# Reading the attention output projection's matrix four rows at a time, with each row still written to its own partition

## The chip, the core and the metric

The kernel runs on one core of one Trainium2 chip. The metric is the device time of one execution in microseconds (us), as a median over several executions.

Two short names help below. A *read* is what a DMA engine fetches from DRAM as one piece, and a *write* is what it puts into on-chip memory (SBUF) as one piece; *descriptor* is the author's word for the entry that describes such a piece; the traces show none. Of the engines, PE multiplies matrices, DVE works on vectors, and SP issues the copies. The trace records DMA *packets*.

## The reference, cut to what matters

```python
def _A_ref(x, k_cache, v_cache, wq, wo):          # decode attention, one query per batch
    ...                                           # window W = 2048 of 8192 positions, 16 KV heads, 32 query heads
    return o.transpose(...).reshape(B, Sq, Hq * Dh) @ wo      # wo: [4096, 576] bf16, 4.7 MB
# b = an MLP of 576 -> 4608 -> 576 with weights w1 and w2;  result = g * a + (1 - g) * b
```

K and V of the window are 134 MB of the 154.3 MB that are read. The output projection `wo` is 4.7 MB, or 3.1%.

## The kernel before

Everything big is loaded by SP's DMA queue, in one stream, into a ring of nine slots of 16 KB per partition. A K or V copy is 2 MB in 128 pieces of 16384 B. After every eighth V copy comes a chunk of `wo`: 1024 rows of 1152 B. Row `128 t + p` goes to partition `p`, block `t`, because that is the layout that the kernel's matmul takes.

```python
WOP, WO_CH, NSLOT = 768, 8, 9     # a block of 576 columns stands every 768 elements; 8 blocks in a chunk
def wo_chunk(i):
    s = take_slot()
    h0 = WO_CH * i
    dst = slot(s)[:, 0:WO_CH * WOP].rearrange("p (t c) -> p t c", t=WO_CH)
    d = dma("sp", lambda e: e.dma_start(dst[:, :, 0:D], A_wo[128 * h0:128 * (h0 + WO_CH), :].rearrange("(t p) c -> p t c", p=128)),
            "s%d" % s, WO_CH * 128 * D * 2, deps=slot_free[s], name="d_wo%d" % i, after=last_dma[-1:])
    last_dma.append(d)
    ...                           # matmuls of the chunk; the slot is free when they are done

def src_of(cache, g, q):          # K and V: 16 KB from each of 32 x 4 places
    hkv, b0 = 2 * g + q // 2, 4 * (q % 2)
    return cache[b0:b0 + 4, hkv, S0:Sk, :].rearrange("a (x r) d -> x a (r d)", x=32)
```

## Time and profile before

| | before |
|---|---|
| time, median | 369.5 us |
| span of the profiled run | 367.9 us |
| DMA queue of SP, packet time as a share of 16 engines' span | 98.9% |
| PE, DVE busy | 72%, 57% |

These are lines of the page of the kernel before. The first two rows have a value for each of 40 equal slices of the span: the busy share of the 16 DMA engines in tenths, and what they moved. Below them are the packets and SP's queue (packets, MB, share).

```profile
DMA  8999999999999999999999999999999999999994
GB/s 345 428 412 424 435 430 433 428 428 428 433 429 431 422 433 426 428 435 427 433 431 433 408 434 432 429 426 433 433 436 428 414 434 424 431 433 440 402 429 193
DMA packets 14923, 154.59 MB, mean 420 GB/s; under 512 B 1292, under 2 KB 5428, under 8 KB 6072
q1 hardware_dynamic: 14848, 154.29, 98.9%
```

The row DMA is full from end to end, so the DMA engines bound this kernel. The table of waits (us in total, times, longest) confirms it from the other side: DVE waits for K.

```profile
DVE arena L642 <- DMA arena<-in_A_k_cache_dram: 60.1, 15, 10.5
```

The timeline of SP around the first `wo` copy (start, duration, instruction): the K copy issued after it holds SP for 18.53 us.

```profile
95.16 0.54 SPq L675 DMA_DIRECT2D arena<-in_A_v_cache_dram  x1
95.74 0.59 SPq L723 DMA_DIRECT2D arena<-in_A_wo_dram  x1
107.98 18.53 SPq L627 DMA_DIRECT2D arena<-in_A_k_cache_dram  x1
126.56 0.82 SPq L675 DMA_DIRECT2D arena<-in_A_v_cache_dram  x1
```

All issues of the `wo` copy together (duration in ns: least, median, most):

```profile
L723 SPq DMA_DIRECT2D arena<-in_A_wo_dram x4: 373/378/586, 95.7 to 314.8; - x4
```

The trace also holds every DMA packet with start, duration and size. Grouped by size, the kernel before has:

```
size      packets   median ns   what
 1152 B     4104         51     rows of wo (4096 of them)
 4608 B      256        178     rest of w1, a part of w2
10368 B      384        389     w2
16384 B     8192        611     K and V
```

### The profile page before, as it was taken

What the parts mean: (1) busy time and instruction counts of PE and PEld (TensorE: products, weight loads), DVE (VectorE), ACT (ScalarE), POOL (GpSimd) and SP (SyncE); (2) the same over time, 40 slices, a digit from 0 to 9 for tenths busy, and PEclk for the clock granted to TensorE, in tenths of its full rate; (3) what the DMA queues carried; (4) which work ended last, traced back from release to release, by engine and by line L of the source; (5) the groups of instructions that cost most, each with busy time, mean ns of one, the idle gap of its engine ahead of it and who ended that gap; (6) DMA issues with size and microseconds to landing.
All of it is one profiled execution on the core that took longest, in us unless ns stands there. A gap on an engine that the chain in (4) does not pass through costs nothing.

```text
span 367.9 us, 4129 instructions
## 1 busy us (share of the span) xinstructions
PE 263.5 (72%) x1837; PEld 87.0 (24%) x1429; DVE 210.4 (57%) x253; ACT 47.8 (13%) x117; POOL 37.5 (10%) x163
## 2 busy tenths in 40 slices
PE   0349984797698589773986399774976398773984
PEld 0339200122132022110321032110321032113542
DVE  0704599699686665459654674469544775364000
ACT  1010000210300220003000310003100300003200
POOL 7020011012011002000101002010110000000000
PEclk9999999699599869887897869886996879886659
DMA  8999999999999999999999999999999999999994
GB/s 345 428 412 424 435 430 433 428 428 428 433 429 431 422 433 426 428 435 427 433 431 433 408 434 432 429 426 433 433 436 428 414 434 424 431 433 440 402 429 193
DMA packets 14923, 154.59 MB, mean 420 GB/s; under 512 B 1292, under 2 KB 5428, under 8 KB 6072
## 3 DMA queue, kind: packets, MB, share of 16 engines
q1 hardware_dynamic: 14848, 154.29, 98.9%
q8 instruction: 13, 0.21, 0.2%
q10 hardware_dynamic: 56, 0.03, 0.0%
q14 instruction: 6, 0.05, 0.0%
HBM read 154.31 MB, written 0.01 MB: 419 GB/s over the span
## 4 chain that ended last, share of the span: by engine, by line
DMA 61%; PE 20%; DVE 16%; SPq 1%; issue 1%; ACT 0%; DVEq 0%; ACTq 0%
DMA arena<-in_A_k_cache_dram 50%; DMA arena<-in_B_w_dram 11%; DVE arena L642 10%; PE ps L173 9%; PE ps L659 3%; DVE arena L587 3%; PE ps L498 2%; PE ps L682 2%; PE ps L697 2%; DVE arena L606 1%; DVE arena L590 1%; PE ps L500 1%; SPq L675 1%; DVE arena L596 0%; SPq L746 0%
## 5 line engine op out<-in xcount | busy, mean ns | idle before, releaser
L642 DVE STREAM_TRANSPOSE arena<-arena 128x2048 f32<-128x2048 f32 x64 | 145.5, 2299 | 71.1 <-DMA arena<-in_A_k_cache_dram 60.1
L173 PE MATMUL ps<-arena 128*128 128x512 bf16 x408 | 141.3, 462 | 0.0
L659 PE MATMUL ps<-arena 128*128 128x512 bf16 x128 | 58.8, 459 | 21.4 <-DVE arena L642 21.3
L691 ACT ACTIVATE arena<-ps 128x512 f32<-128x512 f32 x32 | 19.1, 598 | 196.8 <-PE ps L682 196.8
L659 PEld LDWEIGHTS ps<-arena 128*128 128x128 bf16 x128 | 15.0, 117 | 124.6 <-issue 71.3
L635 POOL COPY arena<-arena 32x32 bf16<-32x32 bf16 x128 | 26.0, 203 | 159.8 <-PE ps L173 145.2
L697 PE MATMUL ps<-arena 128*128 128x8 f32 x256 | 35.3, 269 | 8.7 <-ACT arena L691 7.7
L697 PEld LDWEIGHTS ps<-arena 128*128 128x128 f32 x256 | 34.0, 208 | 21.8 <-ACT arena L691 15.2
L682 PE MATMUL ps<-arena 128*32 128x512 bf16 x512 | 36.4, 410 | 2.9 <-DMA arena<-in_A_v_cache_dram 2.9
L651 PE MATMUL ps<-arena 128*128 128x512 bf16 x8 | 4.7, 585 | 40.8 <-DVE arena L606 40.8
L587 DVE TENSOR_REDUCE arena<-ps 128x1 f32<-128x2048 f32 x8 | 18.3, 2282 | 21.6 <-PE ps L173 21.6
L601 ACT ACTIVATE arena<-ps,arena 128x512 bf16<-128x512 f32 x32 | 21.6, 686 | 40.9 <-DVE arena L596 40.9
L606 DVE STREAM_TRANSPOSE arena<-arena 128x512 bf16<-128x512 bf16 x32 | 19.9, 674 | 0.9 <-ACT arena L601 0.9
L682 PEld LDWEIGHTS ps<-arena 128*32 128x32 bf16 x512 | 11.3, 100 | 37.4 <-issue 27.1
L715 POOL TENSOR_TENSOR arena<-arena 128x16 bf16<-128x16 f32 x15 | 4.0, 266 | 141.7 <-ACT arena L707 141.7
L498 PE MATMUL ps<-arena 128*128 128x8 bf16 x144 | 10.9, 201 | 4.7 <-DMA arena<-in_B_w_dram 4.7
L541 PE MATMUL ps<-arena 128*8 128x288 bf16 (+1 forms) x140 | 11.9, 316 | 2.9 <-DMA arena<-in_B_w_dram 2.8
L498 PEld LDWEIGHTS ps<-arena 128*128 128x128 bf16 x144 | 10.8, 157 | 5.2 <-DMA arena<-in_B_w_dram 5.2
L651 PEld LDWEIGHTS ps<-arena 128*128 128x128 bf16 x8 | 0.9, 107 | 45.1 <-DVE arena L606 45.1
L613 DVE RECIPROCAL arena<-ps 128x32 f32<-128x32 f32 x8 | 2.9, 358 | 13.9 <-PE ps L611 13.9
L420 PE MATMUL ps<-arena 8*128 8x8 bf16 x8 | 0.5, 167 | 13.4 <-DVE arena L393 9.7
L715 DVE TENSOR_TENSOR arena<-ps,arena 128x16 bf16<-128x16 f32 x1 | 0.2, 229 | 16.7 <-PE ps L697 16.7
(83 smaller groups left out, 97.1 us busy)
## 6 DMA issues: line engine op xcount, KB each, us to landing
arena<-in_A_k_cache_dram SPq DMA_DIRECT2D x32, 2048.0 KB, 33.3
arena<-in_A_v_cache_dram SPq DMA_DIRECT2D x32, 2048.0 KB, 34.1
arena<-in_B_w_dram SPq DMA_DIRECT2D x1, 4608.0 KB, 24.3
arena<-in_A_wo_dram SPq DMA_DIRECT2D x4, 1152.0 KB, 36.6
arena<-in_A_wq_dram SPq DMA_DIRECT2D x1, 4096.0 KB, 13.0
arena<-in_B_w_dram SPq DMA_DIRECT2D x3, 1296.0 KB, 14.8
arena<-in_B_w_dram SPq DMA_DIRECT2D x2, 576.0 KB, 20.6
arena<-in_A_wq_dram SPq DMA_DIRECT2D x1, 512.0 KB, 3.6
```

The costliest lines, as they stand in the source:

```text
L173: return e.add_instruction(mybir.InstMatmult(name=nc.get_next_instruction_name(), engine=mybir.EngineType.PE, ins=[e.lower_ap(rhs), e.lowe ...
L498: ins = e.matmul(out_, lhsT, yT[:, kt, :], start=(kt == 0), stop=False)
L541: ins = e.matmul(ps[32 * j:32 * j + 8, BK_ACC, 0:JN], lhsT, rhs[:, JN * j:JN * j + JN], start=False, stop=True, skip_group_check=True, til ...
L587: mx = add("dve", lambda e: e.tensor_reduce(out=k(MX), in_=ps[:, 0:4, :].rearrange("p a n -> p (a n)"), axis=AXL.X, op=ALU.max), deps=[qk_ ...
L601: return e.activation(out=Pm[:, 512 * c:512 * c + 512], in_=ps[:, c, :], func=ACTF.Exp, bias=k(NB), scale=SCALE, accum_out=k(SUM + c))
L606: pts.append(add("dve", (lambda c=c: lambda e: e.transpose(bass.AP(arena, offset=aoffs("PT") + 2048 * (g % 2) + 128 * c, ap=[[AST, 128], [ ...
L635: return e.tensor_copy(dst, src)
L642: tr = add("dve", (lambda h=h, kb=kb: lambda e: e.transpose(bass.AP(arena_f, offset=foffs("KT") + kb * 2048, ap=[[AST // 2, 128], [1, 2048]]),
L659: mm = e.matmul(*args, start=False, stop=last) if rc == 0 else held_matmul(nc, e, *args, stop=last)
L682: mm = e.matmul(ps[c:c + 32, BK_OS[i % 2], :], PT[:, g % 2, 512 * q + 32 * t:512 * q + 32 * t + 32], slot(s)[:, 512 * t:512 * t + 512], st ...
L691: u_ev[i] = add("act", lambda e: e.activation(out=EV[:, i % 2, :], in_=ps[:, BK_OS[i % 2], :], func=ACTF.Copy), deps=[prev] + ([u_sum[i - ...
L697: mm = e.matmul(ps[:, BK_S, OC + 16 * (item % 2) + 8 * (q % 2):OC + 16 * (item % 2) + 8 * (q % 2) + 8], EV[:, i % 2, 128 * r:128 * r + 128 ...
```

## The change

Four consecutive rows of `wo` are contiguous in DRAM. The change reads them as one piece of 4608 B. The four writes of 1152 B that follow must go to four partitions. The change gives the walk of the destination through a shape register, with `run_dma`; in the trace of the changed kernel this is one MOVE_SHAPE more for each copy (24 ns; 375 ns once). The intent is fewer and larger descriptors for the same layout on chip.

```diff
+def run_dma(nc, e, out, in_, shape=None):
+    ...  # turns the walk into numbers
+        kw = dict(dst_dge_shape=enc, bass_dst_dge_shape=tuple(walk))
+    return e.add_instruction(mybir.InstDMACopy(..., ins=e.lower_ap_dma(in_), outs=e.lower_ap_dma(out), **kw))
...
-            d = dma("sp", lambda e: e.dma_start(dst[:, :, 0:D], A_wo[128 * h0:128 * (h0 + WO_CH), :].rearrange("(t p) c -> p t c", p=128)),
+            src = bass.AP(A_wo.tensor, offset=128 * h0 * D, ap=[[4 * D, 32], [128 * D, WO_CH], [1, 4 * D]])
+            d = dma("sp", lambda e: run_dma(nc, e, dst[:, :, 0:D], src, (AST, ((4 * AST, 32), (WOP, WO_CH), (AST, 4), (1, D)))),
```

More of the change, by code (lines that the diff above doesn't have):

```diff
@@ L177, in held_matmul @@
         tile_size=tile_size, tile_position=tile_position, ldweights=False))
+def run_dma(nc, e, out, in_, shape=None):
+    item = 2
+    kw = {}
+    if shape is not None:
+        pst = shape[0]
+        walk = shape[1]
+        enc = []
+        for step, num in reversed(walk[:-1]):
+            parts, rest = divmod(step, pst)
+            assert parts == 0 or rest == 0
+            enc += [parts * 262144 + rest * item, num]
+        enc += [0, 1] * (4 - len(enc) // 2)
+        kw = dict(dst_dge_shape=enc, bass_dst_dge_shape=tuple(walk))
+    return e.add_instruction(mybir.InstDMACopy(
+        name=nc.get_next_instruction_name(), engine=e.engine, queue="qSPDynamicHW", mode="Copy",
+        ins=e.lower_ap_dma(in_), outs=e.lower_ap_dma(out), **kw))
 def build_kernel(nc, A_x, A_k_cache, A_v_cache, A_wq, A_wo, B_x, B_w1, B_b1, B_w2, B_b2, gate_w, out):
```

## The prediction

The sum came to 369.5 - 1.2 = 368.3 us, and the 1.2 us are the choice between 1.7 us, 0.8 us and nothing. The upper end of the range, 370.0 us, allows for causes of a slower time.

> **What bounds the kernel.** The 16 DMA engines. On the page, the row DMA shows nine tenths or more in every slice but the first and last, at 402 to 440 GB/s, and the SP queue's packets take 98.9% of the engines' span of 367.9 us; adding the packets' times up in 2 us steps of the trace, the engines are 99.7% busy from 2 us to 362 us. PE (72%) and DVE (57%) wait for data: in the table of waits DVE waits 60.1 us for K. So packet time saved is span saved.
>
> **What a row costs now.** The trace's DMA packets, grouped by size: 4104 of 1152 B take 51.1 ns each, 4096 of them the projection's rows: 4096 x 51.1 / 16 = 13.1 us of the 16 engines, 3.6% of the span for 3.1% of the bytes. Packets of 4608 B take a median of 178 ns, of 10368 B 389, of 16384 B 611. All fit a rate of 27.2 B/ns plus about 8.6 ns a packet. [...]
>
> **What the change does.** 4096 reads of 1152 B become 1024 of 4608 B; the 4096 writes of 1152 B stay; bytes, layout and order too. If the cost goes with the read, a quad falls from 4 x 51.1 = 204 ns to 178: 1024 x 26.4 / 16 = 1.7 us less. If it goes with the write, nothing. If both carry some, about 0.8 us. I lean to the read, and expect about 1.2 us.
>
> **What it adds.** Four times a shape register is loaded on SP, whose issues of these copies take 0.38 us (median) with slack around them; none of it should reach the critical path. [...]
>
> **The stall on SP.** Each time, the K copy after a projection copy holds SP for 18.5 to 22.3 us (timeline), and the first w2 copy 27 us, until just before the projection packets start (127.8 us for the first). It looks as if its 64 writes per engine fill the queue; K and V have 8. If writes count, the stall stays; I expect this (60%). If it shrinks, issue is earlier, but the engines are already 99.7% busy, so it buys next to nothing.
>
> **Time.** 369.5 - 1.2 = 368.3 us, range 367.3 to 370.0. Faster by over 2%: 0.01; within 2%: 0.97; slower by over 2%: 0.02.
>
> **What would show each step right or wrong.** Right: about 3,000 fewer packets on the page (14923 to about 11850), "under 2 KB" falling from 5428 to about 1350, new 4608 B packets near 178 ns; K, V and w2 packets unchanged at 611 and 389 ns; the row DMA still full. Wrong: 4608 B packets of about 204 ns (the writes carry the cost), or packets still counted as 1152 B at 51 ns.
>
> **What would make the prediction wrong.** [...]the engines run dry around the four projection copies (a dip in the row DMA at 128, 209, 289 and 346 us); fewer than 16 engines used; [...]packets over 204 ns or slower K packets beside them. These make it slower.

## The result

The changed kernel takes 369.19 us (369.02 to 369.38, 5 runs) against 369.51 us (369.37 to 369.71, 5 runs). The ratio is 0.9992, with a 95% interval of 0.998 to 1.0004. A ratio is the mean time of one kernel's fast runs over that of the other's of the same rounds, so it is not quite the ratio of the medians quoted. The gain is about 0.3 us, and its interval includes zero. A change this small has to be judged from packets, which repeat better than the time does: summed up as under x_r1w1 below, the packets of two kernels that move the same pieces in another order agree within 0.02 us (before and e4_split, x_r1w1 and bb_r1w1), while the runs of one kernel spread over some 0.35 us.

These are the same lines of the page after:

```profile
DMA  8999999999999999999999999999999999999994
GB/s 345 428 408 428 428 427 433 432 426 432 435 430 432 422 427 430 432 439 431 426 430 428 422 438 427 430 426 428 433 430 430 428 431 426 433 428 432 418 424 191
DMA packets 11851, 154.59 MB, mean 421 GB/s; under 512 B 1292, under 2 KB 1332, under 8 KB 3000
q1 hardware_dynamic: 11776, 154.29, 98.6%
```

There are 3072 packets fewer, as four reads became one. The bytes are the same, and the engines are still busy throughout. SP's timeline after, in the same stretch:

```profile
94.86 0.53 SPq L693 DMA_DIRECT2D arena<-in_A_v_cache_dram  x1
95.85 0.73 SPq L193 DMA_DIRECT2D arena<-in_A_wo_dram  x1
108.40 0.56 SPq L645 DMA_DIRECT2D arena<-in_A_k_cache_dram  x1
109.01 0.60 SPq L693 DMA_DIRECT2D arena<-in_A_v_cache_dram  x1
```

The long stalls are gone. The K copies after the first three `wo` copies held SP for 18.53, 22.29 and 21.89 us before, and 0.56, 0.54 and 0.53 us after. The issue of the `wo` copies (duration in ns: least, median, most) became dearer, which costs nothing here:

```profile
L193 SPq MOVE_SHAPE arena<-in_A_wo_dram x4: 24/24/375, 95.4 to 314.8; - x4
L193 SPq DMA_DIRECT2D arena<-in_A_wo_dram x4: 707/707/732, 95.8 to 314.9; - x4
```

So stalls of some 60 us in all went away, 3072 packets went away, and the time moved by 0.3 us. Two things in the packet records explain the size. The records do not name the engine, so I joined packets into the succession of one engine by their times; where two engines run in step, the joining can mix them.

**First, packets overlap.** An engine starts the next packet 4 ns before the record of the last one ends. A 51 ns packet starts every 47 ns, a 178 ns packet every 174, and a 611 ns packet every 607. What a packet costs the engine is the distance of starts, not its recorded duration.

**Second, some of the new packets are slow, always in the same places.** These are typical successions of one engine, size:duration in ns, with "x" for repeats; the first is of the kernel before, cut to one engine's 64 rows:

```
before: 16384:611 ... 1152:51 x64                                          16384:611 16384:611 ...
after:  16384:611 ... 4608:178 x11 4608:179 4608:193 4608:194 x3           16384:636 16384:611 ...
```

About the first eleven packets of a copy take 178 ns, the last four about 194, and then the first K packet takes 633 to 641 instead of 611 (some have 616 after it). Over all engines about 30% of the new packets take 184 ns or more, and there are 48 K packets of 630 to 645 ns, 16 for each of the first three copies, where the kernel before has none. 194 ns is a start every 190 ns, or 47.5 ns for each of the four writes. That is what a row cost before.

**Theory A.** A write of 1152 B costs about 47.5 ns, however wide the read was. A wide read can run ahead of its writes, but only until the room between is full. From the after trace this lead is some 11.5 x (190 - 174) = 184 ns, an estimate. Then reads go at the pace of the writes. What this room is, bytes or pieces or time, the trace does not say. When the copy ends, the next K packet waits, and part of the lead is given back.

**Rivals.** D: only the number of reads counts, at 8.6 ns each, as predicted, and something else ate the gain. B: the shape register, or the engines and partitions that it pairs, makes the slow packets (F is its form for the partition steps). C: a fixed number of write descriptors, 48 (the writes of the first twelve packets of the succession above, 12 x 4), is ready beforehand, and the rest comes at 47.5 ns each. E: the gain is the vanished stall.

### The profile page after: what moved, and what is told of

The parts are those of the page before. It is cut to its first block, busy times and chain, and to the rows that moved or that the text cites. A ratio compares the mean times of both kernels' runs of the same rounds, so it can differ in the third digit from the quotient of the medians.

```text
span 367.5 us, 4111 instructions
## 1 busy us (share of the span) xinstructions
PE 254.8 (69%) x1815; PEld 87.3 (24%) x1429; DVE 210.1 (57%) x253; ACT 47.8 (13%) x117; POOL 37.6 (10%) x163
## 4 chain that ended last, share of the span: by engine, by line
DMA 74%; DVE 12%; PE 11%; SPq 1%; ACT 1%; issue 1%; DVEq 0%; ACTq 0%
DMA arena<-in_A_k_cache_dram 50%; DMA arena<-in_B_w_dram 15%; DMA arena<-in_A_v_cache_dram 9%; DVE arena L660 9%; PE ps L173 5%; PE ps L516 2%; PE ps L677 1%; DVE arena L605 1%; PE ps L700 1%; SPq L765 1%; ACT arena L619 1%; DVE arena L624 1%; PE ps L518 1%; PE ps L715 1%; DVE arena L614 0%
## 5 line engine op out<-in xcount | busy, mean ns | idle before, releaser
L173 PE MATMUL ps<-arena 128*128 128x512 bf16 x401 | 134.4, 445 | 15.3 <-DVE arena L660 9.8
L677 PE MATMUL ps<-arena 128*128 128x512 bf16 x115 | 51.8, 450 | 16.7 <-DVE arena L660 16.6
L715 PE MATMUL ps<-arena 128*128 128x8 f32 x256 | 36.9, 275 | 8.7 <-ACT arena L709 7.7
L715 PEld LDWEIGHTS ps<-arena 128*128 128x128 f32 x256 | 35.6, 217 | 22.4 <-ACT arena L709 16.4
L669 PE MATMUL ps<-arena 128*128 128x512 bf16 x6 | 3.5, 585 | 37.8 <-DVE arena L624 37.8
L700 PEld LDWEIGHTS ps<-arena 128*32 128x32 bf16 x512 | 11.3, 100 | 39.8 <-issue 24.1
```

The source lines that it names most:

```text
L173: return e.add_instruction(mybir.InstMatmult(name=nc.get_next_instruction_name(), engine=mybir.EngineType.PE, ins=[e.lower_ap(rhs), e.lowe ...
L677: mm = e.matmul(*args, start=False, stop=last) if rc == 0 else held_matmul(nc, e, *args, stop=last)
L700: mm = e.matmul(ps[c:c + 32, BK_OS[i % 2], :], PT[:, g % 2, 512 * q + 32 * t:512 * q + 32 * t + 32], slot(s)[:, 512 * t:512 * t + 512], st ...
L715: mm = e.matmul(ps[:, BK_S, OC + 16 * (item % 2) + 8 * (q % 2):OC + 16 * (item % 2) + 8 * (q % 2) + 8], EV[:, i % 2, 128 * r:128 * r + 128 ...
```

## The experiments

### Shape registers in new kernels: three that were not run

Three variants of the changed kernel (a shape register with reads of one row, and reads of two and of eight rows) were refused before they reached the chip: new kernels may not set shape registers by hand. They gave no result. What they were to tell is on record, and later runs ask the same questions without the register:

> Shape register kept, but reads go back to one row of 1152 B. Theory A (read overhead is saved, writes stay at about 47 ns each, so reads can only run ahead of writes by some 190 ns per engine and copy): packets back at 1152 B and 51 ns, starting every 47 ns, time as before, 369.5 us within 0.2. If the number of reads fills the queue, the K copy after each projection copy holds SP for 18 to 22 us again; if it was the shape register that removed the stall, it does not. Rival B (the shape register or its engine assignment is what moved the time): time stays at 369.2 us or moves otherwise, or packets differ from 51 ns.

> Two rows per read (2304 B, 2048 packets). Theory A: a read could start every 89 ns, its two writes need about 95, so the lead grows by 6 ns a packet and reaches 190 ns only at the end of the 32 packets of an engine: nearly all packets take 93 ns, no slow ones at the end of a copy; gain much as with four rows, 369.2 us within 0.2. Rival C (the first 48 write descriptors of an engine are ready beforehand, and the rest come at 47.5 ns each): packets slow down to about 99 ns after the 24th of an engine. Rival D (only the number of reads counts, overhead 8.6 ns each): 1.1 us less than before, 368.4 us. Stall on SP: 32 reads per engine, expected short or gone.

> Eight rows per read (9216 B, 512 packets). Theory A: a read could start every 343 ns, its eight writes need about 380; lead of 190 ns is used up after about 5 packets, so packets 6 to 8 of an engine take about 384 ns instead of 347; gain per copy and engine at most 190 ns, as with four rows, 369.2 us within 0.2. Rival D (only the number of reads counts, 8.6 ns each): all packets at 347 ns, 2 us less than before, 367.5 us. Rival C: slow after the 6th packet, so not told apart from A here.

### The old copy in four parts (e4_split)

```diff
-            d = dma("sp", lambda e: e.dma_start(dst[:, :, 0:D], A_wo[... 1024 rows ...]...), ...)
+            for t in range(0, WO_CH, 2):
+                d = dma("sp", ... dst[:, t:t + 2, 0:D], A_wo[... 256 rows ...] ...)
```

> The old copy, in four copies of two heads each, 16 reads and writes per engine in each. Theory A: the 18 to 22 us stalls of SP are gone or short, packets stay at 51 ns, and the time stays at 369.5 us within 0.2, because the engines were busy through the stall anyway. Rival E (the gain of the change came from the stall that vanished): 369.2 us or less.

Measured: 369.66 us (5 runs), ratio 1.0005 (0.9992 to 1.0019). The expectation on the stall was wrong: it only moved, as SP's timeline of this kernel shows.

```profile
95.61 21.65 SPq L724 DMA_DIRECT2D arena<-in_A_wo_dram  x4
117.35 9.02 SPq L627 DMA_DIRECT2D arena<-in_A_k_cache_dram  x1
126.42 0.82 SPq L675 DMA_DIRECT2D arena<-in_A_v_cache_dram  x1
```

The four parts are stuck one behind the other, until the packets of `wo` start at 127.6 us. So the size of one copy is not what holds SP. In all, as many pieces wait as before; reads and writes are equally many here, so this run does not tell which of them count, if it is their number. Of rival E this run says nothing, as the stall is still there.

### Twelve more copies, in three forms (x_r1w1, x_r4w1, x_r4w4)

One copy's gain is below what a time can show, so these kernels add twelve copies of a chunk, spread over the stream, into slots that nobody reads. Results stay correct. The forms differ in the pieces read and written. None uses a shape register; the writes of a read go to one partition, and a copy with differing pieces is made as the instruction, with the two patterns given separately.

```diff
+def copy_as_given(nc, e, out, in_):
+    return e.add_instruction(mybir.InstDMACopy(..., ins=e.lower_ap_dma(in_), outs=e.lower_ap_dma(out)))
+        def wo_again(form):
+            s = take_slot()
+            rows_out = ...  # 128 partitions x 8 blocks of 1152 B, 1536 B apart
+            wide_out = ...  # 128 partitions x 2 blocks of 4608 B, 6144 B apart
+            rows_in = bass.AP(o, offset=0, ap=[[D, 128], [128 * D, 8], [1, D]])
+            four_in = bass.AP(o, offset=0, ap=[[4 * D, 32], [128 * D, 8], [1, 4 * D]])
+            # r1w1: rows_in -> rows_out   r4w1: four_in -> rows_out   r4w4: four_in -> wide_out
+            d = dma("sp", lambda e: copy_as_given(nc, e, dst, src), ..., deps=slot_free[s], ...)
+            slot_free[s] = [d]
```

> The kernel before with 12 more copies of a projection chunk, spread over the stream, into slots that nobody reads (results stay right); each in the old form, 64 reads and 64 writes of 1152 B per engine. This is the yardstick of the next two. All theories: packets of 51 ns every 47 ns, about 3.0 us a copy, so about 369.5 + 12 x 3.1 = 407 us. If the stalls of SP, now 16 instead of 4, run the queue dry, the DMA row dips and it is longer.

> As x_r1w1, but the 12 extra copies read 4608 B and write 1152 B, without a shape register: the four writes go to one partition, 1536 B apart. Theory A (each write of 1152 B takes about 47 ns, so reads only run ahead by some 190 ns per engine and copy, of which the next K packet gives back 25): first 11 packets of an engine 178 ns, the last 194, next K packet about 636; 12 x (0.16 - 0.025) = 1.6 us less than x_r1w1. Rival D (only the number of reads counts, 8.6 ns each, as predicted): 12 x 0.42 = 5 us less. Rival F (the slow packets come from stepping partitions in the shape register walk): no slow packets here, all 178 ns, 12 x 0.22 = 2.7 us less.

> As x_r1w1, but the 12 extra copies read 4608 B and write 4608 B into one partition. Theory A: no write is short, so all packets 178 ns, one every 174 ns, none slow, next K packet 611; 64 x 47 - 16 x 174 = 224 ns less per engine and copy, 12 x 0.224 = 2.7 us less than x_r1w1, a good us less than x_r4w1. Rival D: 5 us less than x_r1w1 and the same as x_r4w1.

All three ran on the same chip in the same rounds:

| | median us (runs) | less than x_r1w1 | sum of packet starts' distances / 16 | less |
|---|---|---|---|---|
| x_r1w1 | 405.77 (4) | | 371.87 us | |
| x_r4w1 | 404.80 (4) | 0.97 us | 370.96 us | 0.91 us |
| x_r4w4 | 403.08 (5) | 2.69 us | 369.16 us | 2.71 us |

The fourth column adds (duration - 4 ns) over all packets of SP's queue of at least 512 B that start after 25 us, and divides by 16 engines. The 128 packets of w1 that end before 28 us are left out, as the limit of 25 us cuts them differently in each trace. For the two kernels of the study the same sum is 335.79 us before and 335.35 after, 0.45 us less, beside a measured 0.3.

When reads and writes are both wide, the gain is 2.69 us, which is what the distance of starts gives: 12 x (64 x 47 - 16 x 174) ns = 2.69 us. (That it fits to the hundredth is luck: the runs of one of these kernels spread over 0.2 to 0.4 us.) All packets of its extra copies take 178 ns. When only the reads are wide, about a third of that is left, and the slow packets are back without a shape register and without stepping partitions: 178 x11, then 184 to 198, then a K packet of 636 ns. That refutes D, which wanted 5 us in both, and it clears the shape register (B, F): slow packets come without it. The gain in time of x_r4w1 was smaller than the 1.6 us expected: in this form many engines turn slow sooner (29 to 75% of a copy's packets take 184 ns or more, against 28 to 35% in the changed kernel); why is open.

The yardstick also bears on the stall. These lines are of the page of x_r1w1 (the row DMA in 40 slices, and the packets), then of its SP timeline:

```profile
DMA  8999999999999999999999999999999999999995
DMA packets 27403, 168.74 MB, mean 418 GB/s; under 512 B 1484, under 2 KB 17908, under 8 KB 18552
```

```profile
48.34 17.10 SPq L635 DMA_DIRECT2D arena<-in_A_k_cache_dram  x1
65.53 3.04 SPq L683 DMA_DIRECT2D arena<-in_A_v_cache_dram  x1
```

The same stretch of x_r4w1, with 16 reads per engine in the copy instead of 64, and the same 64 writes:

```profile
48.37 0.55 SPq L635 DMA_DIRECT2D arena<-in_A_k_cache_dram  x1
52.83 0.53 SPq L683 DMA_DIRECT2D arena<-in_A_v_cache_dram  x1
```

So fewer reads make the stall go away, with a shape register or without. But reads are not all that counts. After the other extra copies of x_r4w1 the next issue was held for up to 7.8 us, and after the last two for 11.3 and 14.2 us; in x_r4w4, with as many reads and only 16 writes, for at most 4.1 us. (Stalls of 17 to 26 us in both follow the four old copies.) In the bursts of bb_r4w1 below, the third copy of each burst was held for 14.0, 26.7, 26.9 and 23.1 us. Counting from the order of issues and the packets' ends, some 76 reads per engine waited when the K copy of the kernel before was let go, but only about 40 when the third copy of a burst was (estimates). So reads alone do not set the limit, and writes alone do not either: in the changed kernel up to 121 writes per engine waited without a stall of over 5 us, and in the kernel before 76 were enough for 18 (the same way of counting). What the limit is stays open. This is the third copy of the second burst in SP's timeline of bb_r4w1:

```profile
154.10 26.69 SPq L181 DMA_DIRECT2D arena<-in_A_wo_dram  x1
```

The stall costs nothing here: in x_r1w1 SP is stuck for most of the span, the row DMA stays full, and twelve copies cost 405.77 - 369.59 = 36.2 us, which is 12 x 64 x 47 ns = 36.1 us of packets and nothing more. E falls.

### A look at other forms (m1_mix)

```diff
-    twelve copies of one form                                        # in words
+    r4w1, r4w2, r4w4, r2w1, r8w1, two r4w1 back to back, r4w2, r4w4, r2w1, r8w1, r4w1, r8w4   # rows per read, rows per write
```

> One look at packets. The kernel before with extra copies of a projection chunk of several forms, into slots nobody reads: read 4608 and write 1152 (once two of these back to back), read 4608 and write 2304, read 4608 and write 4608, read 2304 and write 1152, read 9216 and write 1152, read 9216 and write 4608. Theory A (the lead of reads over writes is limited to about 190 ns, by the amount of data between): read 2304 write 1152 stays at 93 ns to the 32nd packet or nearly; read 9216 write 1152 slows from 347 to about 384 ns after about 5 of 8; read 4608 write 2304 gains lead at some 6 ns a packet and hardly slows; the second of the two copies back to back is slow (194 ns) from its first packet. Rival C (48 write descriptors ready beforehand, the rest at 47.5 ns each): read 2304 write 1152 slows to about 99 ns after 24 packets of an engine; read 4608 write 2304 does not slow at all; the second of the two back to back has fast packets at its start again or is slow throughout.

Durations in ns of one engine's packets in order:

```
read 4608, write 1152   178 x11 179 193 194 194 194
read 4608, write 2304   178 x16
read 4608, write 4608   178 x16
read 2304, write 1152   93 x32                      (one engine of the first copy: the last 18 are 96 98 100 107 in turn)
read 4608, write 1152, two back to back  178 x6 179 185 187 194 x8 ... 194 x10, then K: 636 616
read 9216, write 1152   347 747 748 754 606 707 741 632
```

Pairs stay fast to the end, in both copies, but for one engine. Their lead grows by only 95 - 89 = 6 ns a packet and reaches the limit, if at all, on the last: that is A, and it rules out C, which wanted a change after the 24th packet. The one slow engine starts a packet every 94.6 ns, or 47.3 per write, which again is the pace of the writes; why it came to this after about 14 packets is open. In two copies back to back the second is slow throughout, at a start per 190 ns: the lead is not renewed. These two copies turn slow sooner than a single one, after six or seven packets; why is open.

The packets of 9216 B were a surprise: a few fast ones of an engine at most, then about twice as slow (347 ns, then 606 to 754). Short writes are not the likely cause, as the next look shows with as many outer steps (16): reads of 4608 B took 330 and 346 ns on average with writes of 4608 B, and 315 and 336 with writes of 1152 B.

### How many outer steps the source has (m2_splits)

```diff
-            wide_in: [[r * D, 128 // r], [128 * D, 8], [1, r * D]]          # 8 rows: 16 outer steps
+            wide(r, n): [[r * D, n], [r * n * D, 1024 // (r * n)], [1, r * D]]   # n = 16, 32 or 64 outer steps
```

> One look at packets, extra copies into slots nobody reads, no shape register. The pair of counts that differs from the copies looked at before is the number of steps of the source's outermost dimension: 16, 32 or 64, with the destination's 128 partitions. Theory G ([...]the width of 9216 B was not what made those packets slow): reads of 4608 B with 16 steps are slow, well over 194 ns, near twice 178, whether the writes are 1152 or 4608 B; reads of 9216 B with 32 steps are fast, 347 ns at first and, with writes of 1152 B, about 384 after the fifth of an engine, and with writes of 4608 B 347 throughout; 64 steps as 32. Rival H (reads of 9216 B are slow as such): 9216 B stays at 600 to 700 ns with 32 steps, and 4608 B is fast with 16 steps.

```
read 9216, write 1152, 32 outer steps   347 347 347 347 349 376 382 382
read 9216, write 4608, 32 outer steps   347 x8
read 4608, write 1152, 64 outer steps   178 x6 180 186 188 194 193 194 194 194 193 194
read 4608, write 4608, 16 outer steps   178 178 178 311 406 380 328 329 353 353 299 307 273 281 322 349
```

The times that G foretold came out in every point, and H falls. With 32 outer steps, 9216 B reads are fast, and with one-row writes they turn slow where A says: after five packets, to 382 ns, a start per 378 ns or 47.3 ns per write. With 16 outer steps even 4608 B into 4608 B takes 330 ns on average (346 in a second copy, 315 and 336 where the writes are 1152 B). In the profile it is a dip in throughput with no dip in the busy share. Here are two stretches of this run, the first with the copy of 16 steps, the second with an 8-row copy of 32 steps; the last two columns are the busy share of the DMA engines and GB/s:

```profile
88.00:104.00 16.00, 8.21 (x56) 2.69 (x39) 10.97 (x21) 3.98 (x10) 0.48 (x3) 0.79 1.02 319
60.00:76.00 16.00, 9.68 (x51) 1.97 (x30) 12.77 (x23) 3.38 (x9) 0.88 (x5) 0.79 1.01 429
```

Why 16 steps are slow is not shown: the runs give the times and no cause. The number of steps also changes the distance between the reads in the pattern's second dimension. That distance alone is not the cause: at 128 rows, 9216 B with 16 steps were slow (606 to 754 ns) and 4608 B with 32 steps fast (178 ns; both m1_mix); other effects of the source's addresses are not ruled out. The change, with reads of four rows, has 32 outer steps; reads of eight rows as planned in e3_eight have 16, and eight rows into eight partitions were never run.

### The stall, once more (spread)

```diff
-                    stream.append(("W", chunk))                 # after every eighth V
+                if vi % 8 >= 4:
+                    stream.append(("W", (chunk, quarter)))      # names shortened: a quarter after each of four V; one slot, taken at the first
```

> The kernel before, each projection chunk in four copies of two heads, each after another V copy, so that never more than 16 of its reads per engine wait at once. Theory A (the stalls of SP cost nothing): no stall over a few us after them, packets of 51 ns as before, time 369.5 us within 0.3. Rival E (the gain of the change is the vanished stall): about 369.2 us.

Measured: 380.85 us, ratio 1.0292 (1.0266 to 1.0318), far from both. The edit did more than it was meant to. The slot is taken with the first quarter, but its data are complete only with the last, so the copy that needs this slot nine places later waits for it, and SP with it. The largest wait of SP in this kernel (us in total, times, longest), and two stretches of it (the last columns again busy share and GB/s):

```profile
SPq L153 <- PE ps L541: 85.1, 6, 29.3
140.00:142.00 2.00, 2.00 (x17) 0.55 (x13) 0.68 (x2) 0.00 (x0) 0.62 (x3) 1.00 0.55 229
142.00:144.00 2.00, 2.00 (x17) 0.37 (x6) 1.83 (x1) 0.00 (x0) 0.42 (x3) 1.00 0.07 25
```

L541 is the projection's matmuls. The engines ran dry three times, about 9.7 us in all (the idle shares of 2 us steps added up), and the K and V packets took 1.5 us longer over 16 engines; together that is about the 11.1 us by which the span grew. As a test of E this run is void, and x_r1w1 stands in for it. It does show what a stall of SP costs when the engines *do* run dry.

### Copies in bursts (bb_r1w1, bb_r4w1)

```diff
-    twelve extra copies, one at a time          # in words
+    stream += [("X", form)] * 3      # after every eighth V, four times
```

> The 12 extra copies in the old form, but in four bursts of three back to back. The yardstick of the next run. All theories: packets of 51 ns every 47 ns, about 405.8 us as when spread.

> As bb_r1w1, with the 12 extra copies reading 4608 B and writing 1152 B. Theory A (reads only run ahead of the writes until the room between is full, once per burst): after 7 to 12 fast packets of an engine all others of the burst take about 194 ns; gain once per burst, 4 x 0.08 to 4 x 0.13 = 0.3 to 0.5 us less than bb_r1w1. Rival C2 (the gain is once per copy): 1.0 us less, as with the same copies spread.

Measured: 405.75 us for both medians (4 runs each; means 405.77 and 405.64). By packets (371.86 and 371.68 us) bb_r4w1 needs 0.18 us less. So the gain is not once per copy, which wanted 1.0 us. It is once per burst at most, and smaller than the 0.3 to 0.5 us expected; the times alone could not tell it from nothing. In the trace an engine has about eleven fast packets at the start of a burst and then slow ones to its end:

```
bb_r4w1: 16384:611 x2, 4608: 178 x11 179 194 178 x2 179 193 194 x3 ... 194 x13 192 191 196 194 x13, 16384: 616 611 ...
```

From the mean of these packets (190.6 ns), with 11 of 48 at 178, a slow packet starts about every 190.3 ns, an estimate, where four old rows took 188, so a long burst even eats up part of its lead. In such a burst four-row reads save next to nothing, because the writes set the pace.

## Why the prediction was right or wrong

The predicted time, 368.3 us with a range of 367.3 to 370.0, holds the measured 369.19 us, and "within 2%" was right. The expected gain of 1.2 us was about four times too large, or nearly three by the packets. That the number held was luck as far as the cost of a row goes: the range reached from 2.2 us of gain to 0.5 us of loss, so it would have held with no gain at all.

- **"The 16 DMA engines" bound the kernel: right.** The row DMA is full in both, and the times of all the twelve-copy kernels follow from packet time alone.
- **"27.2 B/ns plus about 8.6 ns a packet": the rate was right, the overhead mis-sized.** The durations overlap by 4 ns. By starts, a packet costs 4.6 ns beyond its bytes (47 - 1152 / 27.2; 607 - 16384 / 27.2 gives the same within 0.1), an estimate at the rate of the prediction. The most that wide reads could bring is 4 x (64 x 47 - 16 x 174) = 896 ns, 0.9 us, not 1.7; x_r4w4 confirms this (2.69 us for twelve copies).
- **"If the cost goes with the read ... with the write ... both": this is where the step failed.** I leaned to the read. The writes of 1152 B carry it, at about 47.5 ns each: with both sides wide twelve copies gained 2.69 us, with wide reads alone 0.97, and in bursts about 0.2. By A, wide reads gain only by running ahead, which by the start distances leaves 64 x 47 - 2850 = some 160 ns per engine and copy, and the next K packets give back 28 ns. Four copies then make about 0.5 us for a typical engine. The sum over all packets says 0.45, and the measured time 0.3, which is within its noise.
- **"4608 B packets near 178 ns" as a sign: true of the median and misleading.** The median was 178 ns; the tail at 194 ns had the answer. The sign named for the opposite case, 204 ns, was computed from overlapping durations and would have been 4 x 47.5 + 4 = 194.
- **"If writes count, the stall stays; I expect this (60%)": wrong.** It vanished. With 16 reads instead of 64 and the same 64 writes the K copies were held for 0.56 us at most. Writes do count elsewhere: after the extra copies with 16 reads per engine the next issue was held for up to 14.2 us with 64 writes (x_r4w1) and for at most 4.1 us with 16 (x_r4w4). What decides when is open. **"It buys next to nothing": right**; x_r1w1 shows that even many more stalls cost nothing.
- **Shape register cost: right that it is harmless**, 24 ns for the register (375 ns once) and 0.71 instead of 0.38 us for the copy.
- **"packets over 204 ns or slower K packets beside them": the second came.** Two of the 1024 new packets took over 204 ns. The K packets of 633 to 641 ns are, by A, the lead given back, and x_r4w1 has them too (636 ns), without a shape register. Packets far over 204 ns came one step further, with 16 outer steps (330 ns for 4608 B); the reason for those was not shown.

## What to carry to other kernels

When descriptors are made larger, ask which side carries the cost: widening the reads while the writes stayed at 1152 B bought here only what reads could run ahead of writes (0.91 us by packets for twelve copies, against 2.71 with writes of 4608 B), and in bursts next to nothing (0.18 us by packets for twelve copies). Cost packets by the distance of their starts on one engine, not by their recorded durations (4 ns longer here), and look at the tail of the durations, not the median alone. A stalled DMA issuer was harmless here as long as the row of the DMA engines stayed full (x_r1w1: 36.2 us for twelve copies, 36.1 of them packets); before spreading copies out to avoid it, check how long their buffers are then held (spread took 380.85 us against 369.51).

No version came out of this that clearly beats both kernels. x_r4w4 shows what remains for `wo`: 0.9 us (an estimate, four times 224 ns), if a layout with four rows per partition can be used, which changes the matmuls; that was not tried.
